# One core of Trainium2, a chunked RWKV-7 recurrence and a mixture of experts: the decay inverses by reciprocal, u solved row-wise and turned, V and u as one stationary operand, and a new written-out order

## The chip, the core and the metric

The kernel runs on one core of a Trainium2 chip. The metric is device time in microseconds (us) of one execution. The kernel before took 685.33 us in the median of 14 runs (680.75 to 689.59).

## The reference

Two blocks stand one behind the other. The first is a recurrence over 768 steps for 4 batches of 8 heads with head dimension 40:

```python
for t in range(S):                                   # S = 768, state is D x D, D = 40
    y[:, :, t] = einsum('bhd,bhde->bhe', rt, state)
    Sa = einsum('bhde,bhe->bhd', state, at)
    state = state * wt[:, :, None, :] - einsum('bhd,bhe->bhde', Sa, bt) + einsum('bhd,bhe->bhde', vt, kt)
```

Its output, read as 3072 tokens of 320 features, goes through a layer of 8 experts. Each token goes to the expert with the largest of its 8 logits: `h = relu(x @ w1[e])`, `y = h @ w2[e]`, with w1 320x1024 and w2 1024x320, times the softmax weight of that expert. Everything is float32.

## The kernel before, in words

**Units.** The recurrence is computed in chunks of C = 64 steps. There are 12 chunks, and each chunk has two units (BH = 2), so 24 units; unit u holds 16 heads as 4 groups (index p) of 2x2 (indices q and par). A tile of 128 partitions has two halves of 64; `mm` multiplies 64x64 blocks in one of the four quadrants of TensorE's array, and `TILES` is the order that visits the four quadrants in turn. A float32 matmul of the code is two MATMUL and two LDWEIGHTS instructions in the trace, so the 16 matmuls of a step are "x32" there.

**One unit.** The decays w come into `dec`. `scan_r` (line 801, VectorE) multiplies them up from the end of the chunk; `recip` (805) takes the reciprocal of the 8 products over the whole chunk; `scan_q` (807) multiplies w up from there, which gives the inverse decays `qq`. `decay_kb` and `decay_a` scale K, B and A. Then TensorE forms the products of A with K and B (`p_a`), and the triangular system (I - N) is inverted by repeated squaring (`p_sq`, `p_sum2`, `p_sum4`, `p_sum8`, `p_last`, the sums by VectorE, `kept` by ScalarE, `tt_add` by GpSimd), which leaves TT; `p_q` corrects it by the block O into Q. The right side `rhs` comes from V and the state (`p_rhs`).

**The part around u.** `p_u1` (line 1014) multiplies rhs as stationary operand by TT into PSUM, with u's features on the partitions; `p_first` (1023) multiplies TT by rhs, with time on the partitions, and `first` brings its negative to x1; `p_u2` (1041) adds x1 times Q to p_u1's sum; `minus` writes -u into slots 0 and 1 of `Vu`, beside V in slots 2 and 3. `p_z` (1051) multiplies V and u, each as a 64x64 stationary block, by R. `t_u` turns u, and two copies `u` put the turned rows into `ZU`. `zu` masks p_z's result into ZU. `p_y` (1072) gives the output and the new state, `xt` and `sa` take them from PSUM, `p_x` (1102) turns the output into token rows and computes the logits.

**Order.** Every piece is a `Step` with an engine, a planned duration and its reads and writes. `in_order` places them greedily by time, but most steps are bound to a written-out order: `FIRST_STEPS` and `LAST_STEPS` list labels for the first and last units on each engine, and `CYCLE` gives, for the units between, a position within the unit for each step and its engine. TensorE, VectorE, ScalarE, GpSimd and SP's DMA queue each execute their list in that order. `keep_warm` (473) puts filler matmuls of the identity in front of a step where the plan has TensorE idle before time `WARM` = 60.

**Behind the units.** `route` counts and ranks the tokens of the chunks by expert; `by_count` orders the experts by size, from which SP learns which expert's weights to fetch next (`order`, `fetch`). `rows_in` gathers token rows by indirect DMA, `p_rows` turns them, `p_h` and `p_z0` are part of the first expert, and after that a plain loop (lines 1534 to 1558) goes over the experts.

Of the kernel before, what the change touches and what calls it, by code (L numbers as in the profile page):

```python
# [23 lines left out]
def kernel(  # L24
# [25 lines left out]
    C = 64  # L50
# [269 lines left out]
    def rows_out(zo, si, alone=False):  # L320
# [5 lines left out]
        if not alone:  # L326
# [14 lines left out]
            p_a:0 t_kb:0 t_v:1 p_sq:0 t_gt:0 t_v:0 p_sum2:0 p_a:1 p_sum4:0 t_kb:1 t_gt:1 p_sum8:0 p_rhs:0 p_sq:1 t_v:2 p_last:0 p_rhs:1 p_sum2:1  # L341
            p_q:0 p_u1:0 p_a:2 p_sum4:1 p_first:0 t_kb:2 p_u2:0 p_sum8:1 p_z:0 p_sq:2 t_u:0 p_last:1 t_gt:2 p_y:0 p_sum2:2 p_q:1 p_u1:1 p_first:1
            p_x:0 t_st:2 p_u2:1 p_rhs:2 p_sum4:2 p_z:1 p_a:3 p_sum8:2 t_u:1 t_kb:3 p_y:1 p_last:2 p_sq:3 p_q:2 p_u1:2 p_first:2 p_sum2:3 p_u2:2
            t_gt:3 p_x:1 p_z:2 p_sum4:3 p_a:4 t_v:3 t_u:2 t_v:4 p_sum8:3 p_y:2 p_sq:4 t_kb:4 t_st:3 p_last:3 p_sum2:4 p_rhs:3 t_v:5 t_kb:5 p_q:3
            p_x:2
        """,
        DVE: """
            zero_dec zero/1 zero/3 zero_dec/1 zero_dec/2 scan_r:0 recip:0 scan_q:0 decay_kb/1:0 decay_a:0 scan_r:1 recip:1 scan_q:1 n1/1:0 n1:0
            t1:0 nkb/1:0 v:1 x0:0 s2/3:0 s2/1:0 decay_a:1 decay_kb/1:1 scan_r:2 x02:0 s2/5:0 s2/4:0 recip:2 scan_q:2 s4:0 x04:0 s4/1:0 n1/1:1 n1:1
            t1:1 s8:0 x08:0 s8/1:0 s2/1:1 s2/3:1 x0:1 decay_kb/1:2 direct:0 direct/1:0 x02:1 s2/5:1 s2/4:1 scan_r:4 scan_r:3 x04:1 s4/1:1 s4:1  # L350
            n1/1:2 n1:2 t1:2 s8:1 s8/1:1 x08:1 zu/1:0 zu:0 s2/1:2 x0:2 s2/3:2 direct:1 direct/1:1 recip:3 xt:0 scan_q:3 s2/4:2 first:1 s2/5:2 x02:2
            decay_kb/1:3 logits:0 x04:2 s4/1:2 s4:2 weight:0 zu/1:1 zu:1 n1/1:3 n1:3 t1:3 x08:2 s8/1:2 s8:2 recip:4 s2/1:3 s2/3:3 scan_r:5 x0:3
            recip:5 nkb:3 x1:3 xt:1 scan_q:4 x12/1:3 x02:3 s2/5:3 s2/4:3 logits:1 zu/1:2 zu:2 x04:3 s4/1:3 s4:3 n1/1:4 weight:1 u/1:2 n1:4 t1:4
            s8/1:3 s8:3 x08:3 sa:2 xt:2 x0:4 nkb:4 scan_r:6 s2/4:4 x02:4 scan_q:5
        """,
        ACT: """
            zero/6 zero/9 first_load/1:0 first_load/3:0 zero/8 zero/4 first_load/1:1 zero/7 first_load/3:1 zero/5 gt/1:0 gt:0 x1:0 off/1:0 off:0
            v/1:1 pc:0 gk:0 zero/10 x12:0 x12/1:0 gt/1:1 gt:1 off:1 nkb:0 x14:0 v:0 v/1:0 x14/1:0 nkb:1 gk:1 off/1:1 pc:1 pc:2 rhs:0 x1:1 v/1:2
            nkb/1:1 rhs:1 x12/1:1 v:2 x12:1 gt:2 q:0 x14:1 gt/1:2 off/1:2 first:0 x14/1:1 off:2 minus:0 nkb/1:2 gate/6 nkb:2 x1:2 u:0 u/1:0 sa0:0
            gk:2 x12/1:2 q:1 x12:2 exp:0 minus:1 rhs:2 x14:2 x14/1:2 sn:2 scaled:0 scaled/1:0 u/1:1 u:1 nkb/1:3 gt:3 off:3 off/1:3 pc:3 gt/1:3  # L360
            kept:2 kept/1:2 q:2 first:2 minus:2 sa0:1 x12:3 gk:3 exp:1 off/1:4 x14/1:3 gt:4 u:2 x14:3 gt/1:4 v:4 v/1:4 scaled/1:1 off:4 v:3
            scaled:1 pc:4 v/1:3 x1:4 nkb/1:4 kept:3 kept/1:3 x12/1:4 x12:4 rhs:3 v:5 sn:3 nkb/1:5 q:3 pc:5
        """,
        POOL: """
            const zero basis/1 basis zero/11 basis/2 basis/3 basis/4 basis/5 const/1 zero/20 const/2 basis/6 gate const/3 basis/7 const/4 basis/8
            basis/9 const/5 zero/12 decay_kb:0 const/6 basis/10 basis/11 zero/19 zero/13 basis/12 basis/13 const/7 basis/14 const/8 zero/18 zero/14
            decay_kb:1 gt_mask:0 s2/2:0 s2:0 zero/15 gate/1 const/9 zero/17 const/10 gate/2 zero/21 gt_mask:1 zero/2 const/11 const/12 decay_kb:2
            decay_a:2 zero/16 s2/2:1 s2:1 zero/22 const/13 const/14 gate/3 gate/4 decay_kb:3 gt_mask:2 s2:2 s2/2:2 const/15 decay_kb/1:4 const/16
            const/17 const/18 const/19 const/20 st:2 decay_a:3 decay_kb:4 s2:3 const/21 s2/2:3 tt_add:2 gt_mask:3 decay_a:4 const/22 decay_kb/1:5
            decay_kb:5 xs_pad:0 const/23 st:3 xs_pad:1 s2:4 s2/2:4 const/24 s2/3:4 s2/1:4 gt_mask:4 const/25 tt_add:3 decay_a:5 st:4 decay_kb:6  # L370
            const/26 decay_kb/1:6
        """,
        SP: """
            first_load:0 first_load/2:0 first_load/4:0 first_load:1 first_load/2:1 first_load/5:1 load:2 first_load/4:1 first_load/5:0 load/3:2
            load/1:2 load:3 load/2:2 load/1:3 load/4:2 load/1:4 load:4 load/2:4 load/2:3 first_load/6:0 load/3:3 gate/5 first_load/6:1 load/1:5
            load/4:4 load:5 load/5:2 load/2:6 load/2:5 load/3:4 load/3:5 load/4:3 load:6 load:7 load/5:3 store:0 load/4:5 load/2:7 load/1:7
            load/1:6 load:8 load/5:4 load/3:6 store:1
# [4 lines left out]
            p_q:20 p_u1:20 p_sum4:21 p_first:20 t_gt:21 t_st:21 p_u2:20 p_a:22 p_z:20 t_u:20 t_st:20 p_x:19 p_sum8:21 p_y:20 p_sq:22 p_last:21  # L382
            t_gt:22 t_kb:23 p_rhs:21 p_q:21 p_a:23 p_sum2:22 p_u1:21 p_first:21 p_u2:21 p_sq:23 p_z:21 t_u:21 p_rows/1 p_sum4:22 p_x:20 p_rows
            p_count:19 p_sum2:23 t_gt:23 p_sum8:22 p_y:21 p_sum4:23 p_last:22 t_v:23 p_x:21 p_rhs:22 p_h p_h/1 p_q:22 p_sum8:23 p_u1:22 p_first:22
            p_h/2 p_h/3 p_u2:22 p_last:23 p_h3 p_rhs:23 p_z:22 p_u1:23 p_q:23 p_first:23 p_count:21 t_st:22 p_h/8 p_u2:23 t_st:23 p_table:19 p_h/9
            p_z:23 p_y:22 p_y:23 p_x:22 p_table:21 p_x:23 p_h/4 p_h/10 p_h/11 p_h/5 p_count:23 p_h/6 p_h/7 p_h3/2 p_h3/1 p_h/12 p_h/13 p_table:23
            p_z0 p_z0/8 p_z0/1 p_z0/9 p_z0/2 p_z0/3 p_h/14 p_z0/10 p_z0/11 p_z0/4 p_z0/12 p_h/15 p_h3/3 p_z0/13 p_z0/5 p_rows/4 p_z0/6 p_rows/2
            p_rows/5 p_z0/14 p_z0/15 p_rows/6 p_z0/7 p_rows/3 p_rows/7
        """,
        DVE: """  # L390
            s2/5:21 x12:21 first:20 s4:21 s4/1:21 x04:21 n1:22 n1/1:22 zu:20 zu/1:20 t1:22 logits:19 s8:21 x08:21 s8/1:21 xt:20 sa:20 scan_q:23
            x0:22 weight:19 nkb:23 q:21 scaled/1:19 n1:23 x12:22 s2/4:22 n1/1:23 t1:23 off/1:23 x02:22 s2/5:22 zu/1:21 x0:23 zu:21 s4/1:22
            logits:20 s4:22 x04:22 weight:20 s2/4:23 x02:23 s2/5:23 s8:22 x08:22 s8/1:22 xt:21 sa:21 direct/1:22 direct:22 logits:21 s4:23 s4/1:23
            x04:23 weight:21 scaled:21 s8/1:23 s8:23 x08:23 relu direct/1:23 direct:23 zu/1:22 zu:22 choose:21 place:21 tab:19 sn:23 one_hots:21
            zu:23 zu/1:23 xt:22 xt:23 tab:21 logits:22 logits:23 choose:23 weight:23 weight:22 place:23 one_hots:23 by_count:23 tab:23 rows_from:23
            in_places:23 rows_from/1:23 rows_to:23 zo/1 rows_to:15
        """,
        ACT: """
            x12/1:21 nkb:22 pc:22 v/1:22 q:20 v:22 x14/1:21 gk:21 minus:20 x14:21 off/1:22 u/1:20 sn:20 sn:21 u:20 gt/1:22 gt:22 exp:19 off:22
            kept:21 kept/1:21 gk:22 nkb/1:23 scaled:19 x1:22 rhs:21 first:21 x12/1:22 gt/1:23 gt:23 minus:21 x1:23 off:23 rows/1 x14/1:22 u/1:21  # L400
            u:21 x14:22 counts:19 exp:20 rows gk:23 scaled/1:20 scaled:20 x12:23 x12/1:23 x14/1:23 v:23 x14:23 exp:21 rhs:22 v/1:23 q:22
            scaled/1:21 first:22 minus:22 rhs:23 relu/1 q:23 first:23 sn:22 minus:23 exp:22 exp:23 scaled:22 scaled:23 scaled/1:22 scaled/1:23
            relu/2 relu/3 relu/4 relu/5 relu/6 relu/7 rows/4 rows/5 rows/6 rows/7 rows/3 rows/2 zo
        """,
        POOL: """
            decay_a:22 rows_in xs_pad:18 s2:22 gt_mask:22 s2/1:22 s2/2:22 tt_add:21 decay_a:23 s2/3:22 rows_in/1 choose:19 xs_pad:19 s2:23 s2/2:23
            s2/1:23 st:22 s2/3:23 gt_mask:23 place:19 xs_pad:20 st:23 one_hots:19 xs_pad:21 xs_pad:22 xs_pad:23 rows_in/2 rows_in/3 rows_in/4
            rows_in/5 rows_in/6 rows_in/7 rows_out rows_out/1
        """,
        SP: """  # L410
            load/4:23 ready:19 load/5:22 store:19 store:18 fetch:18 store:20 store:21 load/5:23 store:22 store:23 order fetch fetch/1 fetch/2
            fetch/3 fetch/4 fetch/5 fetch/6 fetch/7
# [60 lines left out]
    def keep_warm(bank, idle):  # L473
        for i in range(int((idle - (0.25 if idle < 8 else 3.0)) / (0.22 if idle < 8 else 0.27))):
            nc.tensor.matmul(bank[:, :128], lhsT=ident[:], rhs=ident[:], start=True, stop=True, skip_group_check=True)
# [1181 lines left out]
```

## Time and profile before

| What | Value |
|---|---|
| median of 14 runs | 685.33 us (680.75 to 689.59) |
| profiled execution | 680.86 us, its span 679.1 us |
| TensorE busy, weight loads busy | 635.2 us, 506.1 us |
| VectorE, ScalarE, GpSimd busy | 397.0, 288.3, 337.6 us |
| units in a steady cycle | from about 100 to 380 us |
| last chunk, routing, gathers | about 380 to 449 us |
| expert loop | 449 us to the end |

Durations in the text come from the profiled execution, whose own time is 4.5 us under the median of the runs. Busy times overlap between engines. A matmul's duration in the trace holds its latency, about 0.2 us, so that what a step of many matmuls costs TensorE is read from its start to the next step's start.

### The profile page before, as it was taken

Reading aid. Unit: us, or ns where it says so; the run is one execution under the profiler, and the core shown is the slowest. Engines: PE = TensorE matmul, PEld = TensorE weight load, DVE = VectorE, ACT = ScalarE, POOL = GpSimd, SP = SyncE. Lnnn points to the kernel's source line nnn. Section 1 sums busy time; section 2 is a strip of 40 time slices with the busy share of each in tenths; the row PEclk is TensorE's granted clock in tenths of the full one; section 3 lists DMA queues with packets and bytes.
Section 4 is the critical chain, followed back from the end, with each engine's and each line's share of the span. In section 5 each row is a group of like instructions: output and inputs, shape, how many; then the busy total and the mean of one; then the engine's idle time right before and its main releaser. Section 6 shows DMA issues by size and latency. Waiting matters only on the chain. (4 is left out here: it accounts for less than half of the span.)

```text
span 679.1 us, 32215 instructions
## 1 busy us (share of the span) xinstructions
PE 635.2 (94%) x14088; PEld 506.1 (75%) x14088; DVE 397.0 (58%) x851; ACT 288.3 (42%) x745; POOL 337.6 (50%) x508
## 2 busy tenths in 40 slices
PE   7898999999999999999998899789999999999995
PEld 6787889988888888889887888465656565556663
DVE  7799989988888888888887785511101201010110
ACT  5554667666666666667665542121010111111110
POOL 9543667786768677967696660332114012211101
PEclk9999999999999999999999999989999999999998
DMA  4422433334343333333332110638447021125000
GB/s 103 98 50 52 94 84 77 84 79 108 76 102 76 82 83 83 98 72 98 73 89 55 48 57 14 222 113 256 137 131 242 18 101 36 63 94 169 20 8 26
DMA packets 120195, 60.65 MB, mean 89 GB/s; under 512 B 100571, under 2 KB 115934, under 8 KB 120052
## 3 DMA queue, kind: packets, MB, share of 16 engines
q1 hardware_dynamic: 115036, 48.83, 27.1%
q0 software_dynamic: 2976, 9.24, 4.1%
q8 instruction: 111, 1.82, 1.1%
q10 hardware_dynamic: 2040, 0.49, 0.3%
q14 instruction: 32, 0.26, 0.1%
HBM read 49.88 MB, written 8.94 MB: 87 GB/s over the span
## 5 line engine op out<-in xcount | busy, mean ns | idle before, releaser
L1470 DVE TENSOR_SCALAR h_sb<-hp 128x416 f32<-128x416 f32 (+3 forms) x28 | 16.3, 582 | 164.8 <-PE hp L1464 141.6
L745 PE MATMUL ps<-wx 64*64 64x128 f32 (+1 forms) x3072 | 94.5, 259 | 3.1 <-issue 2.1
L877 DVE TENSOR_TENSOR wx<-ps,wx 64x256 f32<-64x256 f32 (+1 forms) x216 | 89.9, 416 | 8.3 <-PE ps L745 4.6
L321 POOL DMA_INDIRECT out_dram<-zo,s_idx x24 | 23.7, 988 | 142.3 <-ACT zo L1487 141.0
L745 PEld LDWEIGHTS ps<-wx 64*64 64x64 f32 x3072 | 77.9, 133 | 10.0 <-issue 7.0
L864 POOL TENSOR_TENSOR wx<-T,ihalf 64x256 f32<-64x256 f32 x88 | 63.7, 724 | 31.2 <-DVE T L860 19.5
L814 POOL TENSOR_TENSOR KB<-KB,rv 128x512 f32<-128x512 f32 x44 | 54.4, 1243 | 23.4 <-PE ps L745 15.1
L734 ACT COPY wx<-ps 128x256 f32<-128x256 f32 (+2 forms) x120 | 46.6, 419 | 40.5 <-PE ps L745 12.9
L910 DVE STREAM_TRANSPOSE wx<-ps 128x512 f32<-128x512 f32 x72 | 50.6, 703 | 6.6 <-PE ps L745 3.9
L1487 ACT COPY zo<-zp 128x320 f32<-128x320 f32 (+1 forms) x24 | 10.2, 425 | 101.5 <-PE zp L1481 97.6
L1471 ACT ACTIVATE h_sb<-hp 128x416 f32<-128x416 f32 (+3 forms) x28 | 14.3, 509 | 87.3 <-PE hp L1464 44.3
L1481 PE MATMUL zp<-wx,h_sb 128*128 128x320 f32 (+3 forms) x176 | 48.5, 433 | 0.0
L1456 PE MATMUL hp<-xgT,w 128*128 128x416 f32 (+1 forms) x128 | 46.6, 512 | 0.0
L1481 PE MATMUL zp<-w,h_sb 128*128 128x320 f32 (+1 forms) x176 | 44.1, 433 | 0.0
L801 DVE TENSOR_TENSOR_SCAN rv<-dec,ones 128x521 f32<-128x521 f32 x24 | 42.5, 1772 | 0.8 <-issue 0.2
L734 ACT COPY ZU<-ps 64x320 f32<-64x320 f32 x90 | 37.8, 420 | 7.6 <-PE ps L854 5.5
L1481 PEld LDWEIGHTS zp<-wx,h_sb 128*128 128x128 f32 (+3 forms) x176 | 30.5, 175 | 13.8 <-issue 0.7
L745 PE MATMUL ps<-ZU,nKB 128*64 128x104 f32 (+1 forms) x768 | 39.5, 254 | 0.6 <-issue 0.4
L1456 PEld LDWEIGHTS hp<-xgT,w 128*128 128x128 f32 x128 | 23.7, 190 | 21.2 <-issue 17.1
L1481 PEld LDWEIGHTS zp<-w,h_sb 128*128 128x128 f32 (+1 forms) x176 | 28.8, 175 | 13.2 <-issue 0.7
L944 POOL TENSOR_TENSOR TT<-TT,wx 128x512 f32<-128x512 f32 x20 | 26.2, 1308 | 23.1 <-ACT TT L734 21.3
L734 ACT COPY nKB<-ps 128x512 f32<-128x512 f32 x44 | 25.9, 589 | 26.7 <-PE ps L975 26.6
(276 smaller groups left out, 1390.1 us busy)
## 6 DMA issues: line engine op xcount, KB each, us to landing
KB<-in_packed_dram SPq DMA_DIRECT2D x184, 40.0 KB
w<-in_moe_w_dram SPq DMA_DIRECT2D x10, 512.0 KB
w<-in_moe_w_dram SPq DMA_DIRECT2D x16, 320.0 KB
x_rows<-xs SPq DMA_DIRECT2D x24, 192.0 KB
A<-in_packed_dram SPq DMA_DIRECT2D x96, 40.0 KB
Vu<-in_packed_dram SPq DMA_DIRECT2D x96, 40.0 KB
R<-in_packed_dram SPq DMA_DIRECT2D x96, 40.0 KB
wx<-in_moe_w_dram SPq DMA_DIRECT2D x12, 320.0 KB
```

The source lines that it names most:

```text
L321: ins_ = nc.gpsimd.indirect_dma_start(out=out[:, :], out_offset=bass.IndirectOffsetOnAxis(ap=si, axis=0), in_=zo, in_offset=None, bounds_c ...
L734: nc.scalar.copy(dst, src)
L745: nc.tensor.matmul(out_, lhsT=lhsT, rhs=rhs, start=start, stop=stop, skip_group_check=True)
L801: Step(turn_of("scan_r", pre + 0.1), DVE, 1.26, lambda e: nc.vector.tensor_tensor_scan(rv[:, : SEG * C1 + 1][:, ::-1], dec[:, ::-1], ones6 ...
L814: Step(turn_of("decay_kb", pre), on_, 1.2 if on_ == POOL else 0.65, lambda e, kb=kb, by=by: any_(e).tensor_tensor(kb, kb, by, op=ALU.mult) ...
L864: Step(turn_of("s2", rk + 0.5), DVE if spread and z else POOL, 0.4 if spread and z else 0.74, lambda e, z=z, par=par, q=q, X=X: any_(e).te ...
L877: nc.vector.tensor_tensor(dst[o_, q], src[o_, q], old[o, q], op=ALU.add)
L910: Step(turn_of(f"x0{k}", rk - 0.4), DVE, 0.72, lambda e, ps=ps, Xn=Xn: nc.vector.transpose(Xn[:, :, :, 0, :], half_sums(ps, 2)[:, :, :, 0, ...
L944: Step(turn_of("tt_add", rk - 1.5), POOL, 1.28, lambda e, X=X, TT=TT: nc.gpsimd.tensor_tensor(TT[:], TT[:], X[:, :, :, 2, :], op=ALU.add), ...
L1456: nc.tensor.matmul(hps[i][:, : c1 - c0], lhsT=w[0][:, db, (fb + i) * 128 : (fb + i + 1) * 128], rhs=xT[:, db, c0:c1], start=(db == 0 and n ...
L1470: nc.vector.tensor_relu(h[:, fb, h0 : h0 + c1 - c0], hps[0][:, : c1 - c0])
L1481: nc.tensor.matmul(zp[r0 : r0 + n], lhsT=h[:, fb, c0 : c0 + n], rhs=w[2][:, fb, :], start=(fb == 0), stop=(fb == FB - 1), skip_group_check ...
```

## The change

1. **Inverse decays.** `scan_q` and the 8 reciprocals go. `recip` now takes the reciprocal of all 128x512 products of `scan_r`, into a ring `q` of 64 columns a head. The ring `qini` and the two memsets of it go; two buffers of a ring `xg` take its place as targets of gathers.
2. **u.** `p_u1` goes. `p_first` leaves its sum in PSUM, and `p_u2` adds Q times x1 to it, with Q stationary; its 16 matmuls now stand in the two quadrants on the diagonal only. So u arrives with time on the partitions: `u` copies it straight from PSUM into ZU, `minus` writes it back to x1, `t_u` turns x1, and a new copy `ut` writes the turned u into Vu.
3. **R.** V goes to slots 2 and 1 of Vu, u to 0 and 3, so that a V and a u lie side by side and `p_z` loads both as one stationary block of 64 rows and 128 columns: 16 matmuls in place of 32.
4. **Routing.** `by_count` waits for the gather indices of `found(1)`, and so stands behind `tab` and `rows_from`. `rows_in` is planned with 2.3, 2.6 and 4.8 us to landing in place of 2.5.
5. **Fillers.** One for every 0.3 us over 0.6 planned, from 0.9 us, in place of one for every 0.22 over 0.25, from 0.45.
6. **Order.** All lists and CYCLE positions are new. In the cycle, one of the two `nkb` copies and `sn` move from ScalarE to VectorE.

```diff
-    Step("recip", DVE, 0.2, reciprocal(qi[:, :, 0], r3[:, :, 1]))
+    Step("recip", DVE, 0.75, reciprocal(qq[:], r3[:, :, 1:]))
-    Step("scan_q", DVE, 1.26, tensor_tensor_scan(qq[:], dec[:, : SEG * C1], qi[:] ...))
...
-    load(SP, 1 + V, lambda q, par: Vu[rows(q), :, 2 + par, :], hV)
+    load(SP, 1 + V, lambda q, par: Vu[rows(q), :, 2 - par, :], hV)
...
-    def p_u1(e):
-        for p in range(NP):
-            for z, q in TILES:
-                mm(t[halves[q], 1 - (z ^ q), p, :], rhs[halves[z], q, p, :], TT[halves[z], q, p, :], start=(p == 0), stop=False)
...
     def p_u2(e):
-        t = pair(psu, C)
+        t = pair(psu, D)
         for p in range(NP):
-            for par, q in TILES:
-                mm(t[halves[q], 1 - par, p, :], x1[halves[par], q, p, :], Q[halves[par], q, p, :], start=False)
-    Step("p_u2", PE, 4 * ROUND, ...)
-    Step("minus", ANY, 0.61, minus(e, Vu[:, :, :2, :] ..., pair(psu, C)))
+            for q in range(2):
+                for h in halves:
+                    mm(t[h, q, p, :], Q[h, q, p, :], x1[h, p, q, :D], start=False)
+    Step("p_u2", PE, 0.6, ...)
+    Step("minus", ANY, 0.44, minus(e, x1q, pair(psu, D)))
+    for h in range(2) if not last else ():
+        Step("u", ANY, 0.44, minus(e, ZU[halves[1 - h], :, h::2, C:], pair(psu, D)[halves[h]]))
+    Step("t_u", PE, 0.44, by_blocks(x1, ps))
+    Step("ut", ANY, 0.61, copy(e, Vu[:, :, ::3, :], ...))
...
     def p_z(e, ps=ps):
         for p in range(NP):
             for par in range(2):
-                for q, i in TILES:
-                    mm(psum[halves[i], ps.at + q, at], Vu[halves[q], p, 1 - par if i ^ par else 2 + par, :], R_[halves[q], p, par, :])
-    Step("p_z", PE, 0.96, p_z, n=128)
+                for q in range(2):
+                    mm(psum[:, ps.at + q, at], Vu[halves[q], p, 2 - 2 * par : 4 - 2 * par, :].rearrange("x a j -> x (a j)"), R_[halves[q], p, par, :])
+    Step("p_z", PE, 0.96, p_z, n=64, shape=WIDE)
...
-    Step("by_count", DVE, 1.3, ..., reads=[h_ptr])
+    Step("by_count", DVE, 1.3, ..., reads=[h_ptr, h_idx[1]])
...
-        for i in range(int((idle - (0.25 if idle < 8 else 3.0)) / (0.22 if idle < 8 else 0.27))):
+        for i in range(int((idle - (0.6 if idle < 8 else 3.0)) / 0.3)):
```

The cycle of TensorE, as the positions order it:

```
before: p_a p_sum4 p_u2 t_st t_v p_z t_u p_sq p_sum8 p_y t_kb p_last p_sum2 p_rhs t_gt p_x p_q p_u1 p_first
after:  p_a p_u2 p_sum4 t_u p_x p_z t_v p_sum8 p_sq p_y p_last p_sum2 t_kb p_rhs p_q t_gt t_st p_first
```

## The prediction

> **What bounds the kernel now.** I read the page first, then the table of busy time by stretches, then TensorE's (PE's) timeline of one unit, its groups by form, the waits, and last VectorE's (DVE's) groups. The first block is a row of the busy line, a row of the DMA queues and two stretches (busy us of PE, PEld, DVE, ACT, POOL, then granted clock):
>
> ```profile
> PE 635.2 (94%) x14088; PEld 506.1 (75%) x14088; DVE 397.0 (58%) x851; ACT 288.3 (42%) x745; POOL 337.6 (50%) x508
> ...
> q8 instruction: 111, 1.82, 1.1%
> ...
> 200.00:250.00 50.00, 47.94 (x1644) 43.49 (x1644) 42.84 (x84) 33.49 (x89) 38.14 (x52) 1.00 0.34 80
> ...
> 400.00:450.00 50.00, 42.84 (x888) 34.36 (x881) 27.52 (x124) 13.46 (x38) 12.18 (x19) 0.93 0.29 94
> ```
>
> PE is the busy engine in the steady part, DVE the next at 43 of 50 us. `xt` of successive units starts at 99.2 and, 17 units on, at 379.0 us: 16.46 us a unit. The expert loop behind 449 us isn't touched. What a step costs PE is the distance between starts in its timeline:
>
> ```profile
> 200.39 1.02 PE L745 MATMUL ps<-turn_gate,xT 128*128 128x88 f32 x8
> 201.34 0.69 PE L745 MATMUL ps<-TT,O 64*64 64x64 f32 x32
> ...
> 205.98 0.72 PE L745 MATMUL ps<-Q,x 64*64 64x64 f32 x30
> 206.63 0.66 PE L854 MATMUL ps<-ident,ST 128*128 128x128 f32 x4
> ...
> 207.65 1.16 PE L745 MATMUL ps<-R,Vu 64*64 64x64 f32 x64
> 208.74 0.66 PE L854 MATMUL ps<-ident,Vu 128*128 128x128 f32 x4
> ...
> 215.95 0.62 PE L745 MATMUL ps<-ZU,Gk 64*64 64x40 f32 x32
> 216.38 0.65 PE L745 MATMUL ps<-ST,A 64*64 64x40 f32 x32
> ...
> 418.73 1.15 PE L745 MATMUL ps<-ZU,nKB 128*64 128x64 f32 x32
> 419.81 0.69 PE L745 MATMUL ps<-R,S 64*64 64x64 f32 x32
> ```
>
> `p_x` is 0.95 us, `p_u2` 0.60 in the median of the units, `p_z` 1.09. Medians over the 17 units: p_a 0.92, the three p_sum 2.63, p_sq, p_last and p_q 1.55, p_rhs 1.02, p_u1 0.47, p_first 0.48, p_u2 0.60, p_z 1.09, p_y 2.15, t_kb 1.02, t_gt and t_st 0.99, t_v and t_u 1.12, p_x 0.95. Sum 14.99. Of the remaining 1.47 us, routing's matmuls take 0.13, and 1.34 is waiting. The waits in this part:
>
> ```profile
> PEld ps L745 <- issue: 14.3, 42, 1.1
> ...
> PE ps L745 <- issue: 7.1, 15, 0.9
> ```
>
> "Issue" means no semaphore. PE's 28,176 instructions over 111 packets of the instruction queue are 254 each, and a packet has 16.4 KB: a page of 256 instructions. In the steady part 73 pages start on average 3.86 us apart, a tenth of them under 3.44, none under 3.32. Of PE's 27 gaps over 0.15 us (13.2 us in all), 20 (9.4 us) end 1.2 to 1.7 us after a page has landed. So PE also runs out of instructions. A unit has 1088, 4.25 pages; at 3.5 us a page that is 14.9 us, as much as the work. I laid pages over the cycle's order with the durations above, each page free to start 3.5 us after the one before: 0.91 us of waiting a unit. That leaves 0.43 for waits on data.
>
> **The change, part by part.** *p_u1 goes:* -0.47 us a unit. *p_z:* 16 matmuls, 32 passes (a load and a multiply each), in two row halves in place of four quadrants, so 16 passes one after another on each half, now as before, but with loads of 128 columns. What a load costs is in the groups of weight loads (mean ns of one before the last bar):
>
> ```profile
> L745 PEld LDWEIGHTS ps<-turn_gate,xT 128*128 128x128 f32 x16 | 1.9, 191 | 0.1
> ...
> L745 PEld LDWEIGHTS ps<-R,S 64*64 64x64 f32 x64 | 1.1, 134 | 0.1
> ...
> L1464 PEld LDWEIGHTS hp<-xT,w1c 64*128 64x128 f32 x8 | 0.6, 186 | 0.2 <-issue 0.2
> ```
>
> A load of 64 rows and 128 columns takes 186 ns, as long as the full one's 191, not the 134 of 64 columns. The multiplies don't set the pace where they are short: p_u1 with 64 columns streamed takes 0.47 us for 8 passes a quadrant, 0.058 a pass, and half of p_rhs (215.95 to 216.38) with 40 streamed takes 0.43. p_x streams 88 columns behind loads of 128 and needs 0.95/8 = 0.119 a pass. So p_z goes from 1.09 to 16 x 0.119 = 1.91, +0.82. Bounds: 0 if a 64-row load is hidden, +0.82; I take the upper, since the 186 ns row has the very shape. *p_u2:* the same 32 passes, but on two diagonal quadrants, so 16 a quadrant in place of 8. The bounds are 0.52 (the count per quadrant doesn't matter) and 1.08 (the row at 418.73: 16 passes on each of two tiles). I take 16 x 0.058 + 0.07 for the start = 1.00, +0.40. PE's work: -0.47 + 0.82 + 0.40 = +0.75, to 15.74 us a unit.
>
> The Trainium skill, "TensorE: Matmul & The Clock Gate", section "LDWEIGHTS (loading the stationary operand)", says that a load costs its columns over 1.2 GHz and that fewer rows save nothing, which speaks against this p_z: by its 107 ns p_z would be 1.71 us, +0.62 in place of +0.82. No run here shows a short multiply behind a 64x128 load.
>
> *Instructions:* p_u1's 64 and half of p_z's 128 go: 960 a unit, 3.75 pages, 13.1 us at 3.5 each. Laid out as above over the new order, waiting for pages falls from 0.91 to 0.45: -0.46. Steady sum: +0.75 - 0.46 = +0.29 us a unit. From 50 us (first `xt`) to 400 us there are 21 units: **+6.1 us**. Bounds a unit: -0.16 (no page waits left) to +0.75 (none saved).
>
> *DVE:* 14.1 us busy a unit (43.2/50 x 16.46). The rows of what goes, and those that show a reciprocal:
>
> ```profile
> L807 DVE TENSOR_TENSOR_SCAN q<-dec,qini 128x520 f32<-128x520 f32 x17 | 23.2, 1366 | 0.6
> ...
> L805 DVE RECIPROCAL qini<-rv 128x8 f32<-128x8 f32 x17 | 2.8, 165 | 0.0
> ...
> L1123 DVE RECIPROCAL g<-g 128x1 f32<-128x1 f32 x16 | 2.6, 164 | 0.5
> ```
>
> scan_q (1.37) and the small reciprocal (0.17) go. The large reciprocal isn't shown; 8 elements take no longer than 1, so I price it like another 512-element pass (`xt` takes 0.68), 0.70, between 0.49 (a memset of 521) and 1.98 (`scan_r` in this part). The copies of `nkb` (0.65 on DVE at 14 us) and `sn` (0.48) come to DVE. Sum: 14.1 - 1.54 + 0.70 + 1.13 = 14.4, at most 15.7: under PE's 16.75, so it costs nothing while PE is the bound. ACT loses 0.59 + 0.44 + 0.16 (a smaller `minus`) and gains `ut`, 0.60: under 11 us. POOL's list keeps its work. SP issues the same loads and stores in a new order, with DMA engines a third busy; nil.
>
> The Trainium skill, "VectorE: DVE Perf Modes", section "First, the fixed hardware budget", says that the reciprocal repeats a divide 8 times; if that were 8 cycles an element, 512 would take 4.3 us (my estimate from its 0.96 GHz) and DVE would need 18.0 us a unit. The rows of 165 and 164 ns speak against it: 7 elements more would show as 58 ns.
>
> *Ramp (0 to 60 us).* PE waits for a PSUM bank and then still plays its fillers with work ready behind them, as at 22.75:
>
> ```profile
> 22.75 2.25 PE L475 MATMUL ps<-ident 128*128 128x128 f32 x18 [2.10 <-DVE qini L805]
> 24.92 1.10 PE L745 MATMUL ps<-wx 64*64 64x128 f32 x32
> ```
>
> From 10.8 us on there are seven more such groups, 8.7 us with this one, about 6 on the chain. By the new formula about half of them go: -3. The first units' chain gains t_u and ut before p_z (see the tail): +1. Ramp **-2.0**, from -6 to +2, as the order of the first steps is new throughout.
>
> *Tail (400 to 449 us).* In the last two units the chain binds, not PE. p_u1 ahead of p_first goes (-0.47); t_u, ut and two handovers come between minus and p_z (0.5 + 0.6 + 0.4), p_u2 +0.40, p_z +0.82, minus -0.16: +2.1, of which I take +1, since two units lie side by side. `by_count` (1.4 us) no longer stands ahead of `tab` and the gather indices: -0.6. Behind it are now SP's `order` and fetch of the second expert's weights, some 2 us later; they were issued by 435.7 us and are used at 462.3, which hides it. The gathers get the DMA engines first, and `p_rows` is reordered around this wait, after which PE ran slower (0.87 against 0.49 us for the three turns at 446.3):
>
> ```profile
> 441.61 0.87 PE L1348 MATMUL ps<-ident,q 128*128 128x128 f32 x3 [4.61 <-DMA q<-x_rows,g_idx]
> ```
>
> -0.4. Tail **0**, from -4 to +4. Total +6.1 - 2.0 + 0 = **+4.1 us**: the profiled execution's 680.9 becomes 685.0, and on the median, which is 4.5 higher, 685.3 becomes 689.4.
>
> **The rivals.** *Pages are the bound and the wide loads hide (faster).* For it: the page rate and the work are equal now, and the plan in the code prices p_u2 at 0.6 and p_z at 0.96. Against: the 186 ns. Then p_z and p_u2 cost what they do today, PE's work falls by 0.47 and page waits by 0.45: -0.9 x 21 - 2 = -21, 664 us; with p_u2 at 1.00 and only p_z hidden, -0.5 x 21 - 2, 673. It decides if p_z's step stays under about 1.5 us. *The new order waits on data (slower still).* Between p_last and p_q PE had p_sum2, p_rhs, t_gt and p_x (3.34 us) to cover `kept` and `tt_add` (0.73 + 0.37 + 1.27 and three handovers, 2.7); now p_sum2, t_kb and p_rhs, 2.92. If these come 0.5 us later than in this trace, every unit waits 0.3, and all in-order work on PE behind p_q with it: +6 on top, 696; with a second such place, 702. *The large reciprocal makes DVE the bound (slower).* At 3 us, above the 1.98 that the rows allow, DVE would reach PE's 16.75; at 3.7 a unit takes 17.4 us, +20 and 705. For it speaks only that no row has a reciprocal of this size.
>
> **How the numbers follow.** Forecast 0.50, hidden loads 0.25, waits 0.20, reciprocal 0.05. The forecast's own range is 680 to 700 (-0.16 to +0.75 a unit, ramp and tail by 2 each). 0.3% (2 us) is what a measurement can tell. Within the forecast 0.32 lie above that, 0.09 within, 0.09 below. Slower 0.32 + 0.25 = 0.57, same 0.09, faster 0.34. The range reaches to 668 (half of the first rival) and 703 (all of the second).
>
> **What would show it.** Right: `ps<-R,Vu` 64*128 x32 near 1.9 us from start to start, `ps<-x,Q` near 1.0, 16.7 us between `xt`, page spacing about 4.4 us, DVE RECIPROCAL 128x512 near 0.7. Wrong: p_z under 1.5; `xt` under 16.3 apart; PE waits on POOL TT; a reciprocal over 2 us.

## The result, and the profile after

The changed kernel takes 720.57 us (median of 10 runs, 714.82 to 726.5) against 685.05 (47 runs of before): a ratio of 1.0516, interval 1.0489 to 1.0543. The forecast was 689.4 with a range of 668 to 703. It said slower, but most of what made the kernel slower wasn't in the forecast.

From the page of the changed kernel: busy time of PE and DVE, the granted clock in 40 slices, the instruction queue, and two groups (busy us in all and mean ns of one behind the first bar).

```profile
PE 658.4 (91%) x12520; PEld 526.3 (73%) x12520; DVE 444.4 (62%) x863; ACT 286.6 (40%) x733; POOL 334.7 (46%) x504
...
PEclk9998899999999999999999999999999999999998
...
q8 instruction: 99, 1.62, 0.9%
...
L801 DVE RECIPROCAL q<-rv 128x512 f32<-128x512 f32 x24 | 80.4, 3351 | 0.7
...
L742 PEld LDWEIGHTS ps<-R,Vu 64*128 64x128 f32 x768 | 45.6, 190 | 5.1 <-ACT wx L731 1.9
```

The large reciprocal takes 3.35 us, not 0.70, and it is VectorE's costliest group but one on the page. The weight load of p_z takes 190 ns, close to the 186 and 191 that the prediction priced it by, and the instruction packets fall from 111 to 99. The same kernel's busy time by stretches (columns as in the prediction):

```profile
50.00:100.00 50.00, 45.74 (x1122) 42.30 (x1115) 40.58 (x72) 24.59 (x66) 21.92 (x27) 0.86 0.24 54
...
200.00:250.00 50.00, 45.30 (x1401) 41.63 (x1403) 46.13 (x80) 29.41 (x79) 34.23 (x54) 1.00 0.34 81
...
400.00:450.00 50.00, 46.86 (x1289) 41.29 (x1285) 40.82 (x85) 24.33 (x63) 29.54 (x57) 1.00 0.17 46
```

In the steady part PE has fallen from 47.9 to 45.3 us of 50 and DVE risen from 42.8 to 46.1. While the pipeline fills, the clock is at 0.86; it was at 1.00. Next PE's and then DVE's timeline of one steady unit (start, length, and in brackets the idle time before and what ended it):

```profile
208.76 0.67 PE L742 MATMUL ps<-TT,O 64*64 64x64 f32 x32
211.08 0.66 PE L847 MATMUL ps<-ident,GT 128*128 128x128 f32 x4 [1.64 <-DVE nKB L733]
...
213.49 1.02 PE L742 MATMUL ps<-x,Q 64*64 64x40 f32 x30
...
216.84 2.00 PE L742 MATMUL ps<-R,Vu 64*128 64x64 f32 x32
218.78 0.66 PE L847 MATMUL ps<-ident,Vu 128*128 128x128 f32 x4
```

```profile
205.81 0.68 DVE L1081 TENSOR_TENSOR xT<-ps,q 128x512 f32<-128x512 f32 x1
206.52 3.35 DVE L801 RECIPROCAL q<-rv 128x512 f32<-128x512 f32 x1
209.79 0.65 DVE L903 STREAM_TRANSPOSE wx<-ps 128x512 f32<-128x512 f32 x1
210.37 0.65 DVE L733 COPY nKB<-ps 128x512 f32<-128x512 f32 x1
...
218.88 1.29 DVE L1053 TENSOR_TENSOR ZU<-ps,m_plus 128x512 f32<-128x512 f32 x2 [0.27 <-PE ps L742]
...
223.43 0.68 DVE L1081 TENSOR_TENSOR xT<-ps,q 128x512 f32<-128x512 f32 x1
224.14 3.35 DVE L801 RECIPROCAL q<-rv 128x512 f32<-128x512 f32 x1
```

These lines hold the steady unit. Behind the reciprocal DVE still has `x02` (the transpose) and the copy of `nkb` to do; that copy frees the PSUM bank that `t_gt` writes, so PE stands from 209.4 to 211.08. From there PE runs without a stop until p_z ends at 218.8; then DVE takes `zu`, sums, `sa` and `xt`, and the next reciprocal starts. From reciprocal to `t_gt` 4.56 us, from there to `zu` 7.80, from there to the next reciprocal 5.26: 17.62 us. `xt` comes every 17.65 us. Neither engine is full (DVE is busy 16.2 us of 17.65); each waits for the other, and both the reciprocal (DVE) and p_z (PE) lie on this loop. PE's waits between 130 and 380 us:

```profile
PEld ps L847 <- DVE nKB L733: 17.7, 10, 1.8
...
PEld ps L742 <- DVE pt__187 L733: 6.2, 4, 1.5
PEld ps L742 <- issue: 3.5, 21, 0.2
```

The long "issue" waits of before (up to 1.1 us) are gone. The second line is the same loop: in four of the fourteen units the copy that PE waits for is a small one of the routing (`pt`), which then stands behind the reciprocal.

### The profile page after: what moved, and what is told of

Same layout as the page of the kernel before. It is cut to its first block, busy times and chain, and to the rows that moved or that the text cites. A ratio compares the mean times of both kernels' runs of the same rounds, so it can differ in the third digit from the quotient of the medians.

```text
span 721.0 us, 29015 instructions
## 1 busy us (share of the span) xinstructions
PE 658.4 (91%) x12520; PEld 526.3 (73%) x12520; DVE 444.4 (62%) x863; ACT 286.6 (40%) x733; POOL 334.7 (46%) x504
## 3 DMA queue, kind: packets, MB, share of 16 engines
q8 instruction: 99, 1.62, 0.9%
## 5 line engine op out<-in xcount | busy, mean ns | idle before, releaser
L731 ACT COPY wx<-ps 128x256 f32<-128x256 f32 (+2 forms) x118 | 48.8, 416 | 81.7 <-DVE wx L903 41.4
L801 DVE RECIPROCAL q<-rv 128x512 f32<-128x512 f32 x24 | 80.4, 3351 | 0.7
L807 POOL TENSOR_TENSOR KB<-KB,rv 128x512 f32<-128x512 f32 x44 | 52.9, 1203 | 34.9 <-PE ps L742 27.4
L742 PE MATMUL ps<-R,Vu 64*128 64x64 f32 x768 | 48.9, 278 | 2.6 <-DVE ZU L739 1.7
L742 PEld LDWEIGHTS ps<-R,Vu 64*128 64x128 f32 x768 | 45.6, 190 | 5.1 <-ACT wx L731 1.9
L1470 PE MATMUL zp<-w,h_sb 128*128 128x320 f32 (+1 forms) x176 | 44.1, 433 | 0.0
L809 POOL TENSOR_TENSOR A<-A,q 128x512 f32<-128x512 f32 x22 | 27.9, 1267 | 33.3 <-DVE q L801 27.6
L1053 DVE TENSOR_TENSOR ZU<-ps,m_plus 128x512 f32<-128x512 f32 x48 | 31.0, 686 | 15.4 <-PE ps L742 15.3
L1445 PEld LDWEIGHTS hp<-xgT,w 128*128 128x128 f32 x128 | 23.7, 190 | 21.2 <-issue 17.1
```

What stands on the lines that cost most here:

```text
L731: nc.scalar.copy(dst, src)
L742: nc.tensor.matmul(out_, lhsT=lhsT, rhs=rhs, start=start, stop=stop, skip_group_check=True)
L801: Step(turn_of("recip", pre - 0.5), DVE, 0.75, lambda e: nc.vector.reciprocal(qq[:], r3[:, :, 1:]), reads=hrv, writes=hq)
L807: Step(turn_of("decay_kb", pre), on_, 1.2 if on_ == POOL else 0.65, lambda e, kb=kb, by=by: any_(e).tensor_tensor(kb, kb, by, op=ALU.mult) ...
L809: Step(turn_of("decay_a", pre), DVE if early else POOL, 0.65 if early else 1.2, lambda e: any_(e).tensor_tensor(Aq[:], Aq[:], qq[:], op=AL ...
L1053: Step(turn_of("zu", rk - 0.8), DVE, 0.69, lambda e, s=s, ps=ps: nc.vector.tensor_tensor(ZU[:, s, :, :C], psum[:, ps.at + s, :].rearrange( ...
```

## The experiments

Each kernel ran beside runs of before on the same chip. Before's own median moved from 679.5 to 692.0 between chips, so small differences are read only between kernels of one chip (the rows with the same "before there"). "Unit" is the mean distance of `xt` from the fifth to the twentieth; "fifth" is the time of the fifth `xt`; "loop" is where the expert loop starts; these three are from one profile each.

| kernel | time | before there | ratio (interval) | unit | fifth | loop |
|---|---|---|---|---|---|---|
| before (profile of the prediction) | 685.05 | | | 16.47 | 114.8 | 449.3 |
| before_again | 679.21 (one run) | 681.22 | | 16.32 | 115.9 | 447.7 |
| changed kernel | 720.57 | 685.05 | 1.0516 (1.0489-1.0543) | 17.65 | 135.1 | 491.2 |
| after_again | 719.14 | 682.12 | 1.0523 (1.0488-1.0558) | 17.65 | 130.7 | 488.5 |
| b_recip | 692.22 | 679.50 | 1.0192 (1.0129-1.0254) | 16.68 | 122.3 | 460.4 |
| a_quad | 700.92 | 679.50 | 1.0294 (1.0223-1.0364) | 17.03 | 126.2 | 469.7 |
| a_scan | 698.82 | 679.50 | 1.0268 (1.0206-1.0331) | 16.28 | 137.0 | 469.6 |
| a_scan2 | 689.34 | 692.04 | 0.9951 (0.9932-0.9970) | 16.49 | 123.0 | 459.1 |
| a_scan2_b | 689.08 | 681.22 | 1.0109 (1.0056-1.0162) | 16.30 | 122.0 | 455.4 |
| a_scan2_quad | 678.62 | 692.04 | 0.9809 (0.9790-0.9828) | 16.18 | 118.6 | 446.5 |
| a_scan2_quad_b | 676.81 | 681.22 | 0.9939 (0.9915-0.9964) | 16.01 | 118.7 | 445.2 |
| a_fill | 722.45 | 692.04 | 1.0442 (1.0376-1.0509) | 17.65 | 134.5 | 490.4 |
| a_late | 751.98 | 692.04 | 1.0868 (1.0848-1.0887) | 19.56 | 133.0 | 518.7 |
| a_nk | 735.71 | 682.12 | 1.0807 (1.0766-1.0848) | 18.64 | 128.7 | 498.5 |
| a_mul | 676.23 | 682.12 | 0.9907 (0.9888-0.9927) | 16.04 | 115.7 | 444.7 |
| a_best | 671.64 | 682.12 | 0.9842 (0.9821-0.9862) | 15.88 | 118.7 | 441.1 |
| a_best_b | 674.36 | 681.22 | 0.9899 (0.9865-0.9932) | 15.86 | 118.9 | 442.6 |

**The operation by itself (probe).** Single operations ahead of the schedule.

> The changed kernel with a row of single VectorE and ScalarE operations ahead of the schedule (reciprocals of 1, 8, 16, 32, 64, 128, 256 and 512 elements on 128 partitions, one of 512 on 64 partitions, a product, a scan, then Ln, Exp and a copy on ScalarE, 512 elements each). If the cost is by the element, 6.5 ns each, 64 elements take 0.42 us, 128 0.84, 256 1.7; 8 elements would take 0.05 us more than one, and only if that is hidden in a fixed cost of some 0.16 us do they show the same. If it is a fixed cost of a large instruction, the widths under 128 all take about 0.17 us. Half the partitions: the same 3.35 us if it goes by the element of a row. Product 0.6 us, scan 1.2 us. Ln and Exp 0.5-0.6 us each.

DVE's timeline of that kernel:

```profile
2.02 0.16 DVE L1380 RECIPROCAL q<-A 128x1 f32<-128x1 f32 x1
2.22 0.20 DVE L1381 RECIPROCAL q<-A 128x8 f32<-128x8 f32 x1
...
3.13 0.55 DVE L1384 RECIPROCAL q<-A 128x64 f32<-128x64 f32 x1
3.72 0.95 DVE L1385 RECIPROCAL q<-A 128x128 f32<-128x128 f32 x1
...
6.50 3.35 DVE L1387 RECIPROCAL q<-A 128x512 f32<-128x512 f32 x1
9.88 3.35 DVE L1388 RECIPROCAL q<-A 64x512 f32<-64x512 f32 x1
13.26 0.69 DVE L1389 TENSOR_TENSOR q<-A 128x512 f32<-128x512 f32 x1
13.99 1.22 DVE L1390 TENSOR_TENSOR_SCAN q<-A 128x512 f32<-128x512 f32 x1
```

From 64 to 512 elements it grows by 2.80 us, 6.25 ns an element, and on 64 partitions it is as long as on 128. So both readings that were expected hold in part: there is a fixed cost of some 0.15 us, and a cost for each element on top. Eight elements cost 40 ns more than one, in a row of 200 ns: too little to set a slope by. On ScalarE Ln and Exp took 0.63 us each, with a table load of 1.28 before each.

**The inverse as before, in the new kernel (a_scan, a_scan2).** The edit (not shown: the buffer of the scan's first values, and a load in SyncE's list that a_scan moves back by one place; a_scan2 moves two early decay loads further back):

```
-  reciprocal(qq[:], r3[:, :, 1:])
+  reciprocal(qi[:, :, 0], r3[:, :, 1])
+  tensor_tensor_scan(qq[:], dec[:, : SEG * C1], qi[:].rearrange("p s j -> p (s j)"), 0.0, mult, add)
```

> The changed kernel with the inverse made as before (8-element reciprocal, then the second scan, both in the place of the large reciprocal); the wide p_z, the new u, the fillers and the order stay. Theory Q (the 3.35 us reciprocal in VectorE's queue is the cause): VectorE's work of a unit falls from 16.1 to 14.0-14.7 us, the steady unit from 17.65 to 16.6-16.9 us, most of the 20 us lost before unit 4 comes back, 688 to 699 us. Theory L (the wider weight loads of p_z and p_u2 are the cause): at most 0.3 us a unit comes back, 712 us or more. Theory F (fewer filler matmuls, cold clock while the pipeline fills): the half-speed stretches at 64-71, 82-88 and 123-126 us stay, and 710 us or more.

> a_scan with two decay loads moved back in SyncE's first list, behind the load of the turn gate: in a_scan they waited there for a buffer that the second scan holds, the turn gate came 6 us late, and TensorE waited 6.6 us for ScalarE at 82 us and fell to half speed. Theory Q (VectorE's 3.35 us is what the ramp lost): the deficit against before at the fourth xt falls from 21.7 to under 8 us, the steady unit stays 16.3, ratio to before 1.005 to 1.015. Theory F (fillers and order, not the reciprocal, lose the ramp): the deficit stays over 12 us, ratio 1.02 or more.

a_scan: 698.8 us, the unit 16.28, under the 16.6 to 16.9 of theory Q, but the fifth `xt` later than in the changed kernel. Its ramp was a fault of the edit: the second scan holds the decay buffer longer, two loads waited for that in SyncE's queue, the turn gate came late behind them, and PE stood in one place:

```profile
82.30 1.83 PE L745 MATMUL ps<-x,Q 64*64 64x40 f32 x30 [6.59 <-ACT x L740]
```

With the two loads behind the turn gate (a_scan2) the time is 689.3 and, on another chip, 689.1 us. The changed kernel took 719.1 to 720.6 and, with other fillers, 722.5 on the first of these two chips: the reciprocal costs 30 to 33 us against the pair that it replaced. a_scan2 is 0.5% faster than before on one chip and 1.1% slower on the other; its own time hardly moved, before's did. At the fourth `xt` it stands at 106.8 and 105.8 us, against 99.2 and 100.8 for before: 5 to 8 us remain lost in the ramp (theory Q expected under 8).

**The same reciprocal in the old kernel (b_recip).**

```
-  Step("recip", ... reciprocal(qi[:, :, 0], r3[:, :, 1]) ...)
-  Step("scan_q", ... tensor_tensor_scan(qq[:], dec, qi, ...) ...)
+  Step("scan_q", ... reciprocal(q3[:, :, :C], r3[:, :, 1:]) ...)
```

> The kernel before with the large reciprocal in the place of its second scan, the 8-element reciprocal left out, and nothing else changed. Theory Q: VectorE's work of a unit rises from 14.1 to 15.6-16.1 us and what stands behind it waits; 700 to 722 us with a steady unit of 17.0-17.7 us, and some half-speed clock while the pipeline fills. Theory L: 680 to 690 us. Theory F: 680 to 690 us, no half-speed clock.

692.2 us, 12.7 more than before: slower, but below the 700 that theory Q expected. The unit rises by 0.2 to 0.4 us only, and DVE is busy 44.1 to 45.5 us of 50 between 150 and 350 us, 15.0 us a unit where the changed kernel has 16.2. One reason is a shorter first scan. In before, between 130 and 380 us, it took 1.95 us on average:

```profile
L801 DVE TENSOR_TENSOR_SCAN rv<-dec,ones 128x521 f32<-128x521 f32 x14 | 27.3, 1950 | 0.4 <-issue 0.2
```

In b_recip it took 1.31, so that the swap adds about 1.0 us of DVE's work a unit and not 1.8.

**p_z in quarters, in the changed kernel (a_quad).**

```
-  for q in range(2): mm(psum[:, ps.at + q, at], Vu[halves[q], p, 2-2*par : 4-2*par, :], R_[halves[q], p, par, :])
+  for q, i in TILES: mm(psum[halves[i], ps.at + q, at], Vu[halves[q], p, 2-2*par+i, :], R_[halves[q], p, par, :])
```

> The changed kernel with p_z issued as 32 matmuls of 64 columns on four quarters of the array, as before, instead of 16 with 128-column weight loads; everything else stays. Theory L: p_z falls from 1.93 to 1.1 us and the unit by 0.4 us or more (32 more instructions of each kind cost some 0.4 of it in page waits): 708 to 714 us. Theory Q: p_z falls too, but TensorE waits for VectorE 1.7 us a unit and the gain goes into that wait: 717 to 724 us.

Both times that were expected were wrong; of theory L only the fall of the unit, by 0.4 us or more, came true. The time is 700.9, ratio 1.0294 against 1.0516, and the unit falls from 17.65 to 17.03, although PE still waits 1.6 us in most units for the copy of `nkb` (PE's waits between 130 and 380 us):

```profile
PE ps L847 <- DVE nKB L733: 17.7, 11, 1.7
PE ps L742 <- DVE pt__187 L733: 4.5, 4, 1.4
```

Where one engine is simply full, a shorter step of another gains nothing. In a loop it can gain its whole length, here 17.62 - 0.84 = 16.8; it gained 0.62 of the 0.84. That fits the loop above.

**A cheap operation in the reciprocal's place (a_mul).**

```
-  nc.vector.reciprocal(qq[:], r3[:, :, 1:])
+  nc.vector.tensor_tensor(qq[:], r3[:, :, 1:], r3[:, :, 1:], op=ALU.mult)
```

> The changed kernel with a product of 512 elements in the place of the large reciprocal: an operation of the price that the prediction put in its sum, 0.69 us. The inverse decays are left out, so what is routed behind is other tokens, and only the time up to the expert loop counts. Theory Q: steady unit 16.2-16.5 us, TensorE over 98% busy there, no half-speed clock between 30 and 430 us, start of the expert loop within 8 us of before's 449. If the new order itself loses time, apart from the reciprocal: unit over 16.7, or start of the expert loop after 460.

> The changed kernel once more, as the yardstick of the three beside it. Theory Q: a steady unit of 17.65 us and 1.6 us of waiting for the copy of nkb in each, as before; 715 to 727 us.

676.2 us beside 719.1: 42.9 us hang on this operation's length. Other tokens are routed, but the expert loop takes 230.1 us in a_mul's profile, 229.6 in after_again's and 229.8 in before's, so the whole times can be compared. Its busy time by stretches and PE's whole list of waits between 130 and 380 us:

```profile
200.00:250.00 50.00, 50.00 (x1521) 46.16 (x1519) 43.09 (x88) 33.60 (x87) 37.27 (x54) 1.00 0.33 78
```

```profile
PE ps L742 <- issue: 0.2, 1, 0.2
```

PE is full and a unit is 16.04 us, its own work: a little under the 16.2 to 16.5 that theory Q expected. The clock fell once between 30 and 430 us, for 3.4 us at 93.4, where it expected no fall. By the loop a unit would need 17.62 - 3.35 + 0.85 (the product's mean there) = 15.1, so the loop no longer binds. Of the 43.3 us between the two profiles' spans 15.0 come before the fifth `xt`, 24.3 in the next 15 units (1.62 each) and 4.5 between there and the expert loop.

**Other places for the work (a_late, a_nk).** a_late puts the reciprocal behind the copy of `nkb` in the steady units (its key from -2.860 to -2.730), a_nk puts that copy on ScalarE:

```
-  "nkb": [(ACT, -1.865), (DVE, -2.740)]
+  "nkb": [(ACT, -1.865), (ACT, -1.860)]
```

> The changed kernel with the large reciprocal one place later in VectorE's steady order: behind the copy of nkb instead of ahead of it and of x02; the first and last lists are the same. If the unit is set by what stands right behind the reciprocal (the bank that nkb frees), TensorE's 1.65 us wait at t_gt goes and the unit falls from 17.65 to 16.3-16.8 us, 13 to 20 us less in all. If it is set by VectorE's sum of 16.1 us in a loop with TensorE, the wait moves to the next step that reads VectorE (the sums, n1) and the unit stays 17.2 to 17.7 us, 0 to 7 us less.

> The changed kernel with the second copy of nkb on ScalarE in the steady units, as before the change, instead of on VectorE right behind the large reciprocal; nothing else is moved. If the unit is set by VectorE's copy that frees the bank for t_gt, TensorE's 1.65 us wait goes, VectorE's work falls from 16.1 to 15.4 us and the unit from 17.65 to 16.3-16.9: 10 to 20 us less than the changed kernel. If the reciprocal only moves the wait on (x02, the sums, decay_a on POOL), the unit stays over 17.2: 0 to 7 us less.

Both expectations failed, in the same direction: 752.0 and 735.7 us, slower than the changed kernel by 29.5 us (beside a_fill on the same chip) and 16.6 us (beside after_again). In a_late PE's wait for `nkb` went, and p_a waits for `decay_a` instead, which needs the reciprocal's result (PE's waits, same stretch; three more, 6.6 us, are put down to the load of A):

```profile
PE ps L742 <- POOL A L809: 20.5, 10, 2.4
```

In a_nk the wait goes to `rhs`. ScalarE's and PE's timelines of one unit, in which the reciprocal runs from 204.60 to 207.96:

```profile
205.65 1.08 ACT L731 COPY nKB<-ps 128x512 f32<-128x512 f32 x2
209.76 0.37 ACT L731 COPY wx<-ps 128x256 f32<-128x256 f32 x1 [3.04 <-DVE wx L870]
210.03 0.43 ACT L731 COPY rhs<-ps 128x320 f32<-128x320 f32 x1
...
210.51 0.68 PE L742 MATMUL ps<-rhs,TT 64*64 64x40 f32 x32 [1.97 <-ACT rhs L731]
```

ScalarE's copy for the sums waits for DVE's sums, which stand behind the reciprocal, and the copy of `rhs` stands behind it in ScalarE's queue. In these two runs the stall passes on from queue to queue instead of going away. Much of their loss is the clock, though. Of the 15 units from the fifth to the twentieth `xt`, 6 in a_nk and 10 in a_late hold a stretch of half speed, where the changed kernel has none. In a_nk these units take 19.5 to 19.6 us and the others 18.0 to 18.1; in a_late they take 20.0 to 20.3 and the others 18.4 to 18.8. So without the clock a unit would still be longer than 17.65, but by less.

**Fillers (a_fill).** The old formula and threshold in the changed kernel.

```
-  for i in range(int((idle - (0.6 if idle < 8 else 3.0)) / 0.3)):
+  for i in range(int((idle - (0.25 if idle < 8 else 3.0)) / (0.22 if idle < 8 else 0.27))):
...
-  if s.n and new and idle > 0.9 and ...
+  if s.n and new and idle > 0.45 and ...
```

> The changed kernel with the filler formula of before (threshold 0.45 us, one matmul per 0.22 us of idle time instead of 0.9 and 0.3); all else stays. Theory F: the half-speed stretches before 127 us shrink from 27 us to under 10, and 8 to 14 us of the 42 come back. Theory Q: the waits behind the reciprocal are not where the plan saw idle time, so few fillers come in the right places; half-speed time falls little, 0 to 5 us come back.

Theory F fell: 722.5 us, unit and `xt` as in the changed kernel (fifth at 134.5, 135.1 without), half speed at nearly the same places (from 63.9, 81.0 and 121.9 us; in the changed kernel from 64.5, 81.6 and 122.6). The old formula does bring more fillers, 138 instructions against 88, but in the trace all of them start before 48 us, since `keep_warm` stops at time 60 of the plan. So the run shows that the change of the formula costs nothing here; whether fillers at 64 to 125 us would have kept the clock up was not tried.

**p_z's loads and the place of p_q, with the cheap inverse (a_scan2_quad, a_best).** a_scan2_quad is a_scan2 with p_z in quarters. a_best also moves p_q's steady key from -0.475 to -0.360, behind `t_gt` and `t_st`.

> a_scan2 with p_z as 32 matmuls on quarters as before. If TensorE's own work sets the unit once the reciprocal is gone, p_z's 0.84 us comes out of the unit and 32 more instructions of each kind cost up to 0.25 us of page waits: unit 15.5 to 15.8 us, 10 to 17 us under a_scan2, which is faster than before. If pages bind, unit 16.1 or more, 0 to 5 us under a_scan2.

> a_scan2_quad with p_q moved in TensorE's steady order from behind p_rhs to behind t_gt and t_st, where p_q's wait for tt_add on POOL (7.4 us between 130 and 380 us) is covered by 1 us more of work. If that wait is the next limit: unit from 16.17 to 15.7-15.9 us, 4 to 8 us less than a_scan2_quad, ratio to before 0.967 to 0.978. If the chain through q and p_u2 then waits instead: no gain, 0.979 to 0.985.

> The kernel before, once more with its profile, on the chip of the three beside it. If the chips differ in how fast TensorE's instructions arrive, the waits without a releaser (issue) and the steady unit (16.46 us) move together, with the same durations of the operations; if they differ in the clock, the durations move.

> a_scan2 again, beside the next two. Steady unit 16.3-16.5 us, 687 to 691 us; to before 0.990 to 1.010, as the chip has it.

> a_scan2_quad again, on the same chip. p_z's wide loads, theory L: 8 to 13 us under a_scan2 (0.84 us less work a unit, of which 0.3 to 0.5 go into waiting for tt_add).

> a_best again, on the same chip. p_q's wait for tt_add covered: 4 to 8 us under a_scan2_quad; if that difference came from the chip, 0 to 2 us.

On one chip 689.1, 676.8 and 674.4 us: the wide loads cost 12.3 us (10.7 on the other), the place of p_q 2.4. The unit of the second is 16.01 us, not the 15.5 to 15.8 expected: p_q now waits for `tt_add`, half a microsecond a unit. PE's waits between 130 and 380 us, first of a_scan2_quad_b and then of a_best_b:

```profile
PE ps L745 <- POOL TT L945: 8.1, 11, 1.0
```

```profile
PE ps L745 <- POOL TT L945: 0.3, 1, 0.3
```

The wait is gone, but the unit fell by 0.15 us only and the time by 2.4 us, less than the 4 to 8 that were expected. PE's longest "issue" row rose from 0.7 to 3.4 us in the same stretch; where the rest of the gain went isn't shown.

a_best is faster than before by 1.6% and 1.0% on the two chips that it ran on, and than the changed kernel by 47.5 us on the chip where both ran. It keeps the u summed in PSUM, the routing, the fillers and the new order but for p_q, and gives up the large reciprocal and the wide p_z. before_again has a unit of 16.32 instead of 16.47 us, with 2.6 us less waiting on "issue" in PE's longest row between 130 and 380 us (4.2 against 6.8). That fits a difference in how PE's instructions arrive, for part of before's spread between executions. Why it took 692 us on one chip stays open: there is no profile of before from that chip.

## Why the prediction was wrong, point by point

- **The large reciprocal, priced 0.70 us, took 3.35.** This is the step that failed. It rested on two rows, 165 ns for 8 elements and 164 for one; at 6.25 ns an element the difference is 44 ns, and from one unit to the next the 8-element operation took anything from 160 to 206 ns in before, and 197 on average in a_scan2. The rows were the nearest in kind but much too small to carry a slope to 512. The upper bound of 1.98 us was a scan's, another operation, so the range was not a bound on this one. With an operation near the assumed length (a_mul, 0.85 us) the change is faster than before by 0.9%, so "slower" came true by luck, not by the sum that gave +4.1 us.
- **The page that was set aside**, of the Trainium skill ("VectorE: DVE Perf Modes", "First, the fixed hardware budget") was nearer: my estimate from its repeat count of 8 was 4.3 us, measured 3.35.
- **The third rival had the mechanism, with a chance of 0.05, but was mis-sized.** It let DVE bind alone: at 3.35 us that gives a unit of 17.0 (14.1 - 1.54 + 3.35 + 1.13). (43.2/50 x 16.46 is 14.2, not 14.1; the trace has 14.13 from the fifth to the twentieth `xt`, so the sum stands.) Measured 17.65, as the two engines wait for each other on a loop, and 15 to 20 us more before the fifth `xt`, where the rival had nothing.
- **p_z 1.91, p_u2 1.00:** 1.93 from start to start (216.84 to 218.78 is 1.94), and about 0.9 (0.80 for 30 of the 32 matmuls). Both near. PE's work was near too: 15.74 and 0.13 of routing were forecast, and a_mul, where PE is full, has 16.04. The price of the wide loads, +0.82 us a unit, shows as 12.3 us in all on one chip and 10.7 on the other, where 24 units make 20: p_q's wait for `tt_add` (8.1 us against 1.5 between 130 and 380 us) takes most of the rest.
- **Instruction pages:** predicted 0.45 us a unit of waiting, and 0.43 for data. In a_mul both are near nothing, so the waiting that went is some 1.3 us a unit, not 0.46; how much of it is the new order and how much the 960 instructions wasn't separated. With 16.04 us in place of 16.32 to 16.47 a steady unit is 0.3 to 0.4 us shorter where +0.29 was predicted. This is the second term that was mis-sized.
- **Ramp -2, tail 0:** the fifth `xt` came 20.3 us late (after_again: 15 to 16). a_mul, at 115.7 us against 114.8 and 115.9, shows that it is the reciprocal. Part of it comes by way of the clock: the changed kernel's profile has 17.1 us at half speed between 60 and 130 us, after_again's 6.8. Fewer fillers were to bring 3 us; a_fill, with its first `xt` at 56.9 us against 57.4 to 57.6, shows nothing of that size. From the twentieth `xt` to the expert loop a_mul takes 88.5 us, before 87.4: the tail was right but for 1 us.
- **The second rival's place, p_last to p_q,** didn't wait in the changed kernel. It does as soon as the reciprocal and the wide p_z are gone (8.1 us in 250, a_scan2_quad_b).

The reciprocal costs 12.7 us in the old order and 30 to 33 in the new. Why it costs more there isn't shown. The new order puts the copies of `nkb` and `sn`, 1.1 us, on DVE as well, one of them behind the reciprocal, and was written for a reciprocal that the code plans at 0.75 us; but a_nk, which takes one of the copies away again, is slower still. Whether an order found with 3.35 us would lose less was not tried.

## What to carry to other kernels

Don't carry the price of an operation from a handful of elements to hundreds: where no row shows it at its size, look for what its kind does for each element, and let the range hold that. When two in-order engines hand work to each other once in each unit, add up the loop through both, handovers included: while the loop is what binds, an operation on it can cost up to its whole length (0.62 of 0.84 us in a_quad), though neither engine is full. And when a reordered kernel is slower, put a cheap operation in the suspect's place first: it separates the operation from the order in one run.

## What the runs showed of the hardware

- Reciprocal on VectorE, f32: 0.16 us for one element, 0.55 for 64, 3.35 for 512, the same on 64 and on 128 partitions. A product of 512 took 0.69, a scan 1.22.
- The granted clock changed on a grid of 3.41 us. In a_nk the half-speed stretches between 130 and 400 us start at 171.4, 191.8, 284.0, 321.5, 359.1 and 396.6 us, all close to whole multiples of 3.41 apart, and last 3.4 us. PE's wait of 1.97 us that ended at 171.37 lay inside one step of the grid and half speed followed. The one of the same length that ended at 210.51 lay across two and nothing followed. In the changed kernel's steady units waits of 1.64 us had no such effect. Over the steps of the grid between 130 and 400 us in the changed kernel, a_nk and a_late, half speed followed every step in which PE was idle for 1.83 us or more and none with 1.65 or less; of three steps with 1.70 to 1.74 us it followed one. The limit is thus near half of a step. The Trainium skill ("TensorE: Matmul & The Clock Gate", section "What's actually happening") names a free-running window of 3413 ns, which agrees; it asks for at least one idle window, and here 1.97 us idle in one were enough.
- The first scan (521 elements) took 1.95 us on average in before's steady part, 1.31 in b_recip, which has before's order, and 1.24 to 1.44 in the kernels with the new order, with operands of the same size. In the changed kernel's steady part the scans without a GpSimd instruction beside them all took 1.24 us and the three with one 1.43; in before all of them had one. Whether that is the cause was not tested.
